# A fused attention and two-product MLP in fp32 pairs: the image's low half taken from PSUM, the weights' conversion moved into a PSUM bank, four units between products

## The chip, the cores and the metric

One core of a Trainium2 chip runs the whole program. The metric is the device time of one execution in microseconds; times below are from the hardware profiler or are medians of several executions.

## The reference

Attention with queries averaged in pairs, its output laid out as 2304 tokens of 512, and then a two-product MLP without a gate. Weights and activations are fp32 values (the weights come as float64).

```python
q_pool = q.reshape(B, H, S // 2, 2, D).mean(axis=3)          # B, H, S, D = 4, 8, 1152, 64
attn = softmax(q_pool @ k.T / sqrt(D))
x = (attn @ v).transpose(0, 2, 1, 3).reshape(B * S // 2, H * D)   # 2304 x 512
h = x @ w_in                                                  # 512 x 2048
g = s * maximum(h, 0) ** 2 + b                                # s, b: one number each
out = g @ w_out                                               # 2048 x 512
```

## The kernel before

**Pairs.** To keep fp32 accuracy every matrix operand is a pair: a high part rounded to the engine's fp32r format, and a low part, what rounding took away. A product is three multiplications: high by high, high by low, low by high.

**Attention** runs first, for 32 heads, and ends near 572 us. The change leaves it as it is. Its output `x` goes to DRAM (`xd`), block by block.

**The MLP** works on 9 blocks of 256 tokens and 16 slices of 128 hidden columns. A *unit* is one block by one slice, 144 in all, in three passes over the blocks: slices 0 to 2, 3 to 8, 9 to 15 (`SW`). One block in one pass is a *sweep*: 3, 6 or 7 units. For each unit, on the engine in brackets:

- `mm1`, the **first product** (TensorE): 12 multiplications of 256 columns into the left half of a PSUM bank `h`;
- **relu** L277 (ScalarE): `r`;
- **square** L267 (VectorE): `t` = max(h, 0) times `r`, into SBUF;
- the **image**, twice (ScalarE): L270 makes `gh`, s t + b rounded to fp32r; L271 makes the same in full, `g`, in the right half of the bank `h`;
- **rest** L274 (VectorE): `gl` = `g` - `gh`; it is the last reader of the bank `h`, of which there are four;
- `mm2`, the **second product** (TensorE, L287): 6 multiplications of 512 columns into two banks `y`, `DEPTH` = 3 units after the first product.

After the last unit of a sweep `store` takes `y` out: L294 (ScalarE) in the first pass, L296 (VectorE, with the sum of the pass before, `yq`) in the others.

**The order** is written out by hand. After each first product and after each half of a second product the loop calls `pace`, one *tick*, so a unit has three. `later(k, fn)` puts a step k ticks later; steps that are due are issued in the order in which they were put down. The engines run what they were given in that order. `MO` = (2, 3, 6) places square, image and rest.

**The split of x.** At a sweep's start the next block's `x`, already fetched (`xr`, one buffer, on SP's queue), is copied to its high part (L198, ScalarE, one tick later) and the low part is taken (L239, GpSimd, two ticks later). After that the block after the next is fetched.

**The conversion of weights.** Slices 3 to 15 of both matrices are converted from float64 while the first units run, 26 *chunks* of 128 by 512, one every `WB` = 6 ticks; slices 9 to 15 are wanted first at unit 81. A chunk's steps, at the ticks in `STB`, are: L144 and L145 (ScalarE) from the two words of a double; L149, L151, L152 (VectorE), clamp, shift and merge, each needing the one before; L155 (VectorE) and L156 (ScalarE, the high part); L160, L163, L166 (GpSimd): the scaled low word, the difference from the high part, their sum. All tiles are in SBUF, and each exists twice.

Of the kernel before, what the change touches and what calls it, by code (L numbers as in the profile page):

```python
# [38 lines left out]
XT = (1, 2, 3, 5, 8)  # L39
SW = (3, 9)  # L40
CB, CP = 274, 18
WB = 6
# [12 lines left out]
def attention_moe_kernel(ctx: ExitStack, tc: tile.TileContext, q, k, v, w_in, w_out, s_in, b_in, out):  # L55
# [46 lines left out]
            wo_hi[f] = oh[:, i, :]  # L102
            wo_lo[f] = ol[:, i, :]

    def conversions(pool, stage, f0, f1, bufs, stages):

# [29 lines left out]
        def narrow(i):  # L136
            _, hi, lo, name = chunks[i]
            words = raw.pop(i).rearrange("p c (n w) -> p c n w", w=2)
            high, low = words[:, :, :, 1].bitcast(F32), words[:, :, :, 0].bitcast(U32)
            hm, ab, A, R = (tmp(t, name) for t in ("whm", "wab", "wA", "wR"))  # L140
            hmi, abi, Ai, top = (t.bitcast(I32) for t in (hm, ab, A, high))

            def s0():
                nc.scalar.activation(hm, high, AF.Abs)  # L144
                nc.scalar.activation(R, low, AF.Copy, scale=2.0 ** -52)  # L145

            def s1():

                nc.vector.tensor_scalar(out=hm, in0=hm, scalar1=W_MIN, scalar2=W_MAX, op0=ALU.max, op1=ALU.min)  # L149

                nc.vector.tensor_scalar(out=abi, in0=hmi, scalar1=0x07FFFFFF, scalar2=3, op0=ALU.bitwise_and, op1=ALU.logical_shift_left)  # L151
                nc.vector.scalar_tensor_tensor(out=Ai, in0=top, scalar=-0x40000000, in1=abi, op0=ALU.bitwise_and, op1=ALU.bitwise_or)  # L152

            def s2():
                nc.vector.tensor_scalar(out=abi, in0=Ai, scalar1=-0x800000, scalar2=None, op0=ALU.bitwise_and)  # L155
                nc.scalar.activation(hi, A, AF.Copy)  # L156
# [61 lines left out]
    class Moe:  # L218
# [33 lines left out]
        def mm1(self, blk, f):  # L252
            xh, xl = self.x[blk]
            h = self.hp.tile([P, 512], F32, tag="h", name=f"h{blk}_{f}")
            n = 0
# [468 lines left out]
```

## Time and profile before

| what | value |
| --- | --- |
| median of 3 runs | 1018.68 us (1016.87 to 1018.93) |
| the profiled execution's own time | 1018.46 us |
| its span, first to last instruction | 1016.6 us |
| TensorE busy | 927.6 us, 91% |
| VectorE busy | 651.7 us, 64% |
| ScalarE busy | 686.6 us, 68% |
| GpSimd busy | 379.6 us, 37% |

PE is TensorE's multiplications, PEld its weight loads, DVE VectorE, ACT ScalarE, POOL GpSimd, SP the queue that issues the transfers. A row `out<-in` names the tiles without their numbers; `x4` counts instructions; what stands in brackets behind a row is the idle time before it and what ended it. In the list of waits the columns are total us, times, longest us. Busy shares average over stages; here the attention (up to 572 us) and the three passes of the MLP have different limits.

### The profile page before, as it was taken

How to read it: one execution, taken by the hardware profiler on the slowest of the kernel's cores; microseconds unless marked ns; L12 is line 12 of the kernel's file. 1: busy time of each engine (PE TensorE's matmuls, PEld its weight loads, DVE VectorE, ACT ScalarE, POOL GpSimd, SP SyncE). 2: the span in 40 equal slices, each digit the busy share in tenths (PEclk: the TensorE clock that was granted, in tenths of full speed). 3: DMA queues.
4: the chain of work that ended last, by engine and by line, in shares of the span. 5: the costliest groups of instructions: out<-in, count | busy, mean ns of one | idle time of the engine just before them, and what ended most of it. 6: DMA issues, size and time to landing. Idle time of an engine off the chain costs nothing.

```text
span 1016.6 us, 16051 instructions
## 1 busy us (share of the span) xinstructions
PE 927.6 (91%) x5680; PEld 818.0 (80%) x5680; DVE 651.7 (64%) x1191; ACT 686.6 (68%) x1278; POOL 379.6 (37%) x270
## 2 busy tenths in 40 slices
PE   4899999999999999989989987888889999999998
PEld 2778888888788878878878876767779999999997
DVE  5677777777778777877876378777783333333333
ACT  2577677767776787778777777876666555555553
POOL 5323223423342335235523288786772010011000
PEclk9999999999999999999999999999999999999999
DMA  8769765876587669766762245554442313213211
GB/s 166 137 117 190 152 124 108 179 158 126 114 165 161 122 136 184 167 125 136 175 154 55 74 148 186 185 187 145 141 149 84 125 63 114 73 63 92 96 43 42
DMA packets 255311, 131.15 MB, mean 129 GB/s; under 512 B 203776, under 2 KB 227328, under 8 KB 255232
## 3 DMA queue, kind: packets, MB, share of 16 engines
q1 hardware_dynamic: 248064, 130.06, 53.5%
q10 hardware_dynamic: 7168, 0.08, 0.4%
q8 instruction: 45, 0.74, 0.3%
q14 instruction: 34, 0.28, 0.1%
HBM read 68.68 MB, written 18.87 MB: 86 GB/s over the span
## 4 chain that ended last, share of the span: by engine, by line
PE 56%; DVE 20%; ACT 12%; issue 5%; DMA 2%; POOL 2%; ACTq 1%; SPq 0%; DVEq 0%; POOLq 0%
PE y L287 13%; PE h L258 12%; PE s L472 10%; PE o L501 7%; PE m L442 6%; DVE pl L484 4%; DVE pm L443 3%; PE o L511 3%; PE o L509 3%; ACT s L482 3%; ACT ph L480 3%; PE o L507 2%; DVE wAo L152 2%; DVE wAi L152 2%; DVE wabo L151 1%
## 5 line engine op out<-in xcount | busy, mean ns | idle before, releaser
L443 DVE TENSOR_REDUCE pm<-m 128x1 f32<-128x384 f32 x432 | 230.1, 548 | 51.1 <-PE m L442 44.0
L472 PE MATMUL s<-qq,kk 128*128 128x288 f32 x1152 | 208.0, 307 | 18.1 <-DVE pl L484 16.0
L258 PE MATMUL h<-x,wih 128*128 128x256 f32 x1152 | 213.3, 282 | 3.7 <-POOL x L239 3.7
L472 PEld LDWEIGHTS s<-qq,kk 128*128 128x128 f32 x1152 | 170.8, 190 | 40.9 <-DVE pl L484 16.6
L258 PEld LDWEIGHTS h<-x,wih 128*128 128x128 f32 x1152 | 186.9, 189 | 16.6 <-POOL x L239 5.5
L484 DVE TENSOR_TENSOR pl<-s,ph 128x576 fp32r<-128x576 f32 x176 | 132.5, 753 | 85.9 <-ACT s L482 85.8
L442 PE MATMUL m<-kh,qz 128*128 128x384 f32 x384 | 167.5, 446 | 21.5 <-DVE pm L443 21.0
L267 DVE SCALAR_TENSOR_TENSOR t<-h,r 128x256 f32<-128x256 f32 x144 | 60.7, 421 | 168.3 <-ACT r L277 168.3
L480 ACT ACTIVATE ph<-s 128x576 fp32r<-128x576 f32 x176 | 113.9, 647 | 79.6 <-PE s L472 78.6
L258 PE MATMUL h<-x,wil 128*128 128x256 f32 x576 | 162.2, 282 | 0.0
L239 POOL TENSOR_TENSOR x<-xr,x 128x1024 fp32r<-128x1024 f32 x27 | 66.0, 2444 | 229.6 <-ACT x L198 229.6
L501 PE MATMUL o<-pe,vf 128*128 128x288 f32 x448 | 144.7, 407 | 0.0
L287 PE MATMUL y<-woh,gl 128*128 128x512 f32 x288 | 115.7, 402 | 24.9 <-DVE gl L274 24.9
L270 ACT ACTIVATE gh<-t,sb 128x256 fp32r<-128x256 f32 x144 | 86.2, 598 | 65.9 <-DVE t L267 65.8
L482 ACT ACTIVATE s<-s 128x576 f32<-128x576 f32 x176 | 114.2, 649 | 0.0
L287 PE MATMUL y<-wol,gh 128*128 128x512 f32 x288 | 113.2, 393 | 0.0
L287 PE MATMUL y<-woh,gh 128*128 128x512 f32 x288 | 112.8, 392 | 0.0
L258 PEld LDWEIGHTS h<-x,wil 128*128 128x128 f32 x576 | 109.5, 190 | 0.0
L442 PEld LDWEIGHTS m<-kh,qz 128*128 128x128 f32 x384 | 74.7, 195 | 43.1 <-DVE pm L443 33.9
L507 PE MATMUL o<-ph,vv 128*128 128x288 f32 x352 | 107.4, 305 | 0.2 <-POOL vv L200 0.2
L509 PE MATMUL o<-ph,vl 128*64 128x288 f32 x352 | 104.5, 297 | 0.9 <-POOL vl L417 0.9
L511 PE MATMUL o<-pl,vv 128*128 128x288 f32 x352 | 103.6, 294 | 0.0
(73 smaller groups left out, 1481.9 us busy)
## 6 DMA issues: line engine op xcount, KB each, us to landing
kk<-kh SPq DMA_DIRECT2D x32, 576.0 KB, 5.7
kraw<-in_k_dram SPq DMA_DIRECT2D x64, 144.0 KB, 3.1
qraw<-in_q_dram SPq DMA_DIRECT2D x128, 72.0 KB, 2.5
vf<-in_v_dram SPq DMA_DIRECT2D x32, 288.0 KB, 4.4
kk<-kT SPq DMA_DIRECT2D x32, 288.0 KB, 3.3
qq<-qh SPq DMA_DIRECT2D x64, 144.0 KB, 5.6
xr<-xd SPq DMA_DIRECT2D x18, 512.0 KB, 4.0
wsti<-in_moe_w_in_dram SPq DMA_DIRECT2D x16, 512.0 KB, 4.8
```

Of the source, the lines that this page charges most:

```text
L258: nc.tensor.matmul(h[:, :TB], st[:, c, :], mv[:, c, :], start=(n == 0), stop=(n == 3 * NC - 1))
L287: nc.tensor.matmul(y[:, :DM], st[:, ts_], mv, start=(first and n == 0), stop=(last and n == 2))
L442: nc.tensor.matmul(ps[:, :KB], st, khs[p][:, e * KB:(e + 1) * KB], start=True, stop=True)
L443: nc.vector.tensor_reduce(out=pms[p][:, col, e:e + 1], in_=ps[:, :KB], axis=AX.X, op=ALU.max)
L472: nc.tensor.matmul(ps[:, a, :HALF], kk[:, i, j * P:(j + 1) * P], qq[:, i, a], start=(i == 0), stop=(i == 1))
L480: nc.scalar.activation(ph, ps[:, :, :HALF], AF.Exp, scale=SCALE)
L482: nc.scalar.activation(ps[:, :, :HALF], ps[:, :, :HALF], AF.Exp, scale=SCALE)
L484: fresh.append(lambda: eng.tensor_tensor(out=pl, in0=ps[:, :, :HALF], in1=f32(ph), op=ALU.subtract))
L501: nc.tensor.matmul(o[:, :HALF], vfs[hd % 2][:, j], ph[:, a], start=first, stop=last)
L507: nc.tensor.matmul(o[:, :HALF], vv[:, j], ph[:, a], start=first, stop=False)
L509: nc.tensor.matmul(o[0:D, :HALF], vl[:, j], ph[:, a], start=False, stop=False)
L511: nc.tensor.matmul(o[:, :HALF], vv[:, j], pl[:, a], start=False, stop=last)
```

## The change

- **The image's difference.** The square now multiplies by s as well and is written into the right half of the bank `h` (L273). One image is left (L276, `gh` = square + b), reading PSUM; the rest (L279) adds b to the square in PSUM and subtracts `gh` in one operation. The second image and the SBUF tile `t` are gone.
- **The conversion on one PSUM bank.** ScalarE writes |high word| into a bank of its own (L148); clamp, shift and merge (L156, L158, L159) work in place there; the exponent mask (L162) and the high part (L163) are read from it; the difference from the high part (L170) moves from GpSimd to VectorE. The scaling of the low word (L152) moves from ScalarE to GpSimd. There is one such bank, for 26 chunks.
- **Wider steps.** The first 12 chunks come every 7 ticks and the others every 11 (`WB`), and a chunk's steps are closer together (`STB`).
- **Banks and distance.** Three `h` banks for four, and four units between a unit's products (`DEPTH`), with five buffers of `gh` and `gl`.

```diff
-WB = 6
+WB = (7, 11)
-STB = (0, 2, 4, 6, 8, 10)
+STB = (0, 2, 3, 5, 5, 8)
-DEPTH = 3
+DEPTH = 4
...
+            bank = None if psum is None else psum.tile([P, 512], F32, tag="w", bufs=1, name=f"w{name}").rearrange("p (c f) -> p c f", c=NC)
+            hm, bits, full = (hm, ab, A) if psum is None else (bank, bank, bank)
+            eng = nc.gpsimd if psum is None else nc.vector
...
-                nc.scalar.activation(R, low, AF.Copy, scale=2.0 ** -52)
+                if psum is None:
+                    nc.scalar.activation(R, low, AF.Copy, scale=2.0 ** -52)
+                else:
+                    nc.gpsimd.tensor_scalar(out=R, in0=low, scalar1=2.0 ** -52, scalar2=0.0, op0=ALU.mult, op1=ALU.add)
...
-                nc.gpsimd.tensor_tensor(out=A, in0=A, in1=f32(hi), op=ALU.subtract)
+                eng.tensor_tensor(out=A, in0=full, in1=f32(hi), op=ALU.subtract)
...
-            t = self.p.tile([P, TB], F32, tag="t", bufs=2, name=f"t{blk}_{f}")
-            g = h[:, TB:]
+            t = h[:, TB:]
...
-                nc.vector.scalar_tensor_tensor(out=t, in0=h[:, :TB], scalar=0.0, in1=r, op0=ALU.max, op1=ALU.mult)
-                nc.scalar.activation(gh, t, AF.Identity, bias=sb[:, 1:2], scale=sb[:, 0:1])
-                nc.scalar.activation(g, t, AF.Identity, bias=sb[:, 1:2], scale=sb[:, 0:1])
+                nc.vector.scalar_tensor_tensor(out=t, in0=h[:, :TB], scalar=sb[:, 0:1], in1=r, op0=ALU.mult, op1=ALU.mult)
+                nc.scalar.activation(gh, t, AF.Identity, bias=sb[:, 1:2])
...
-                nc.vector.tensor_tensor(out=gl, in0=g, in1=f32(gh), op=ALU.subtract)
+                nc.vector.scalar_tensor_tensor(out=gl, in0=t, scalar=sb[:, 1:2], in1=f32(gh), op0=ALU.add, op1=ALU.subtract)
...
-    ps_h = ctx.enter_context(tc.tile_pool(name="ps_h2", reuse_waits="tile", bufs=4, space=PSUM))
+    ps_h = ctx.enter_context(tc.tile_pool(name="ps_h2", reuse_waits="tile", bufs=3, space=PSUM))
+    ps_w = ctx.enter_context(tc.tile_pool(name="ps_w2", reuse_waits="tile", bufs=1, space=PSUM))
...
-        if count % WB == 0:
+        if wait == 0:
             weights_b()
-        count += 1
+            begun += 1
+            wait = WB[0 if begun <= 2 * (SW[1] - SW[0]) else 1]
+        wait -= 1
```

How the instructions move, at three places. The first is VectorE in the first pass, one chunk between units: before (`whm`, `wab`, `wA` are the chunk's tiles in SBUF),

```order
L267 SCALAR_TENSOR_TENSOR t_1_7049<-h_1_7035,r_1_7048 128x256
L149 TENSOR_SCALAR whmi_7055<-whmi_7055 128x512
L151 TENSOR_SCALAR wabi_7056<-whmi_7055 128x512
L152 SCALAR_TENSOR_TENSOR wAi_7057<-wsti_6965,wabi_7056 128x512
L274 TENSOR_TENSOR gl_0_7013<-h_0_6997,gh_0_7012 128x256
L155 TENSOR_SCALAR wabi_7056<-wAi_7057 128x512
L267 SCALAR_TENSOR_TENSOR t_2_7089<-h_2_7075,r_2_7088 128x256
L274 TENSOR_TENSOR gl_1_7051<-h_1_7035,gh_1_7050 128x256
```

and now, where `wo` is the bank and `h_0_6957`, `h_1_7007` are units 9 and 10:

```order
L273 SCALAR_TENSOR_TENSOR h_0_6957<-h_0_6957,sb,r_0_6970 128x256
L279 SCALAR_TENSOR_TENSOR gl_2_6942<-h_2_6927,sb,gh_2_6941 128x256
L156 TENSOR_SCALAR wo_6987<-wo_6987 128x512
L158 TENSOR_SCALAR wo_6987<-wo_6987 128x512
L159 SCALAR_TENSOR_TENSOR wo_6987<-wsto_6902,wo_6987 128x512
L162 TENSOR_SCALAR wabo_6984<-wo_6987 128x512
L273 SCALAR_TENSOR_TENSOR h_1_7007<-h_1_7007,sb,r_1_7020 128x256
L279 SCALAR_TENSOR_TENSOR gl_0_6972<-h_0_6957,sb,gh_0_6971 128x256
L170 TENSOR_TENSOR wAo_6985<-wo_6987,woh_6656 128x512
```

The mask L162 now stands directly behind the three steps, ahead of the next square and of the rest of unit 9, and a fifth operation, L170, follows that rest.

The second is ScalarE at a sweep's first unit in the first pass. Before,

```order
L277 ACTIVATE r_0_7259<-h_0_7246 128x256
L156 ACTIVATE wih_6651<-wAi_7218 128x4x128
L198 ACTIVATE x_6_6_7244<-xr_6_7151 128x1024
L270 ACTIVATE gh_0_7261<-t_0_7260,sb 128x256
L271 ACTIVATE h_0_7246<-t_0_7260,sb 128x256
L277 ACTIVATE r_1_7297<-h_1_7284 128x256
```

and now:

```order
L282 ACTIVATE r_0_7317<-h_0_7304 128x256
L205 ACTIVATE x_7_7_7302<-xr_7_7220 128x1024
L299 ACTIVATE yo_True_False<-y_0_7249 128x512
L299 ACTIVATE yo_True_False<-y_1_7250 128x512
L148 ACTIVATE wo_7345<-wsto_7254 128x512
L276 ACTIVATE gh_0_7318<-h_0_7304,sb 128x256
L282 ACTIVATE r_1_7364<-h_1_7351 128x256
```

With one unit more between the products, the two copies of `y` (L294, now L299) fall between the split of `x` and the image of the sweep's first unit; before they stood two units later.

The third is GpSimd, between two splits of `x`. Before,

```order
L239 TENSOR_TENSOR x_4_4_6996<-xr_4_6902,x_4_4_6995 128x1024
L160 TENSOR_TENSOR wRo_6970<-wRo_6970,wabo_6968 128x512
L163 TENSOR_TENSOR wAo_6969<-wAo_6969,woh_6653 128x512
L166 TENSOR_TENSOR wol_6654<-wAo_6969,wRo_6970 128x512
L160 TENSOR_TENSOR wRi_7058<-wRi_7058,wabi_7056 128x512
L163 TENSOR_TENSOR wAi_7057<-wAi_7057,wih_6651 128x512
L239 TENSOR_TENSOR x_5_5_7116<-xr_5_7025,x_5_5_7115 128x1024
```

and now:

```order
L246 TENSOR_TENSOR x_4_4_6956<-xr_4_6872,x_4_4_6955 128x1024
L167 TENSOR_TENSOR wRo_6986<-wRo_6986,wabo_6984 128x512
L152 TENSOR_SCALAR wRi_7067<-wsti_6982 128x512
L173 TENSOR_TENSOR wol_6657<-wAo_6985,wRo_6986 128x512
L246 TENSOR_TENSOR x_5_5_7075<-xr_5_6992,x_5_5_7074 128x1024
```

The subtraction is gone from this queue, a scaling stands in it, and fewer of them lie between two splits.

Lines move by the added text: L258 to L265 (first product), L277 to L282 (relu), L287 to L292 (second product), L294 and L296 to L299 and L301, L198 to L205, L239 to L246, L160 and L166 to L167 and L173. The prediction uses the old numbers for rows of the kernel before and the new ones for what is new.

## Rows read from the trace of the kernel before

**Rows 1.** The page's strip of 40 slices of 25.4 us: busy tenths of TensorE.

```profile
PE   4899999999999999989989987888889999999998
```

**Rows 2.** Busy time of each engine in two stretches (columns: stretch, its length, PE, PEld, DVE, ACT and POOL busy us with instruction counts, granted clock, DMA share, GB/s).

```profile
572.00:760.00 188.00, 159.40 (x980) 135.65 (x979) 144.25 (x220) 137.36 (x274) 140.17 (x91) 1.00 0.49 159
765.00:1005.00 240.00, 240.00 (x1546) 218.87 (x1545) 80.51 (x198) 134.55 (x272) 28.85 (x12) 1.00 0.25 80
```

**Rows 3.** The chain of waits in order of time (start, us, what): the first product with which the chain stays on TensorE, and the last two pieces.

```profile
759.55 1.41 PE h L258 x12
...
1006.10 1.43 PE h L258 x12
1007.53 5.47 PE y L287 x24
```

**Rows 4.** The timeline of TensorE (start, us): the first product of the MLP, and a wait in unit 6.

```profile
572.05 0.40 PE L258 MATMUL h<-x,wih 128*128 128x256 f32 x2
...
586.68 0.39 PE L258 MATMUL h<-x,wih 128*128 128x256 f32 x1 [0.41 <-POOL x L239]
```

**Rows 5.** What TensorE waited for from 572 to 760 us (total us, times, longest us).

```profile
PE y L287 <- DVE gl L274: 24.9, 17, 1.7
PE h L258 <- POOL x L239: 3.7, 6, 0.9
```

**Rows 6.** The timeline of VectorE (start, us): one chunk of the conversion.

```profile
643.88 0.43 DVE L149 TENSOR_SCALAR whmo<-whmo 128x512 f32<-128x512 f32 x1
644.41 1.33 DVE L151 TENSOR_SCALAR wabo<-whmo 128x512 int32<-128x512 int32 x1
645.83 1.60 DVE L152 SCALAR_TENSOR_TENSOR wAo<-wsto,wabo 128x512 int32<-128x512 int32 x1
647.35 0.41 DVE L274 TENSOR_TENSOR gl<-h,gh 128x256 fp32r<-128x256 f32 x1
647.69 0.41 DVE L155 TENSOR_SCALAR wabo<-wAo 128x512 int32<-128x512 int32 x1
```

**Rows 7.** Shortest, median and longest time in ns of VectorE's operations, by line, and the first and last start. In L484, L267, L274 and L296 one operand (`s`, `h`, `h`, `y`) lies in PSUM; in the others all lie in SBUF.

```profile
L151 DVE TENSOR_SCALAR wabo<-whmo x16: 426/1330/1405, 419.6 to 755.0; 128x512 int32<-128x512 int32 x16
...
L152 DVE SCALAR_TENSOR_TENSOR wAo<-wsto,wabo x16: 691/693/1643, 420.1 to 756.4; 128x512 int32<-128x512 int32 x16
...
L155 DVE TENSOR_SCALAR wabo<-wAo x16: 409/792/2283, 422.8 to 758.2; 128x512 int32<-128x512 int32 x16
...
L484 DVE TENSOR_TENSOR pl<-s,ph x175: 739/757/759, 27.5 to 567.2; 128x576 fp32r<-128x576 f32 x175
...
L267 DVE SCALAR_TENSOR_TENSOR t<-h,r x144: 386/424/426, 575.4 to 1008.0; 128x256 f32<-128x256 f32 x144
...
L274 DVE TENSOR_TENSOR gl<-h,gh x144: 407/414/425, 577.6 to 1009.6; 128x256 fp32r<-128x256 f32 x144
...
L296 DVE TENSOR_TENSOR yo_False_True<-y,yq x18: 681/691/692, 859.9 to 1013.0; 128x512 f32<-128x512 f32 x18
```

**Rows 8.** Groups of VectorE's instructions from 572 to 760 us (busy us, mean ns of one; idle before): a chunk's four operations, for `w_out`.

```profile
L152 DVE SCALAR_TENSOR_TENSOR wAo<-wsto,wabo 128x512 int32<-128x512 int32 x13 | 15.3, 1179 | 1.1
...
L151 DVE TENSOR_SCALAR wabo<-whmo 128x512 int32<-128x512 int32 x13 | 13.8, 1058 | 1.3
...
L155 DVE TENSOR_SCALAR wabo<-wAo 128x512 int32<-128x512 int32 x13 | 12.9, 992 | 0.0
...
L149 DVE TENSOR_SCALAR whmo<-whmo 128x512 f32<-128x512 f32 x13 | 11.0, 846 | 1.8
```

**Rows 9.** Groups of ScalarE's instructions over the whole run (busy us, mean ns of one; idle before).

```profile
L270 ACT ACTIVATE gh<-t,sb 128x256 fp32r<-128x256 f32 x144 | 86.2, 598 | 65.9 <-DVE t L267 65.8
...
L277 ACT ACTIVATE r<-h 128x256 f32<-128x256 f32 x144 | 54.4, 378 | 59.5 <-PE h L258 58.9
...
L156 ACT ACTIVATE woh<-wAo 128x512 fp32r<-128x512 f32 x16 | 10.1, 630 | 17.6 <-DVE wAo L152 15.3 <-POOL wAi L163 2.4
...
L294 ACT ACTIVATE yo_True_False<-y 128x512 f32<-128x512 f32 x18 | 9.6, 583 | 0.0
```

**Rows 10.** Groups of GpSimd's instructions over the whole run (the same columns).

```profile
L166 POOL TENSOR_TENSOR wol<-wAo,wRo 128x512 fp32r<-128x512 f32 x16 | 22.6, 1414 | 0.9
...
L163 POOL TENSOR_TENSOR wAo<-wAo,woh 128x512 f32<-128x512 f32 x16 | 21.8, 1362 | 0.0
...
L200 POOL TENSOR_SCALAR vv<-vf 128x576 fp32r<-128x576 f32 x32 | 21.5, 673 | 96.7 <-DMA vf<-in_v_dram 51.0 <-PE m L442 16.7 <-PE o L511 14.8
L160 POOL TENSOR_TENSOR wRo<-wRo,wabo 128x512 f32<-128x512 f32 x16 | 21.4, 1338 | 10.3 <-DVE wabo L155 9.8 <-DMA wsti<-in_moe_w_in_dram 0.4
```

**Rows 11.** The split of `x`: from the timelines of SP, ScalarE and GpSimd (start, us), and the fetches of 512 KB from 570 to 760 us (count, size, median us from issue to landing).

```profile
577.49 0.91 SPq L230 DMA_DIRECT2D xr<-xd  x2
...
583.09 1.06 ACT L198 ACTIVATE x<-xr 128x1024 fp32r<-128x1024 f32 x1 [1.13 <-DMA xr<-xd]
...
584.23 2.40 POOL L239 TENSOR_TENSOR x<-xr,x 128x1024 fp32r<-128x1024 f32 x1 [5.37 <-ACT x L198]
...
616.95 2.67 POOL L239 TENSOR_TENSOR x<-xr,x 128x1024 fp32r<-128x1024 f32 x1 [1.18 <-ACT x L198]
...
627.47 2.41 POOL L239 TENSOR_TENSOR x<-xr,x 128x1024 fp32r<-128x1024 f32 x1 [2.24 <-ACT x L198]
...
xr<-xd SPq DMA_DIRECT2D x8, 512.0 KB, 4.1
```

More of the change, by code (lines that the diff above doesn't have):

```diff
@@ L103, in weight_tiles, with conversions @@
             wo_lo[f] = ol[:, i, :]
-    def conversions(pool, stage, f0, f1, bufs, stages):
+    def conversions(pool, stage, f0, f1, bufs, stages, psum=None):
         weight_tiles(pool, f0, f1)
@@ L139, in narrow @@
             high, low = words[:, :, :, 1].bitcast(F32), words[:, :, :, 0].bitcast(U32)
[L140 to L141 removed]
+            hm, ab, A, R = (tmp(t, name) for t in ("whm", "wab", "wA", "wR")) if psum is None else (None, *(tmp(t, name) for t in ("wab", "wA", "wR")))
+            bank = None if psum is None else psum.tile([P, 512], F32, tag="w", bufs=1, name=f"w{name}").rearrange("p (c f) -> p c f", c=NC)
+            hm, bits, full = (hm, ab, A) if psum is None else (bank, bank, bank)
+            hmi, biti, abi, fulli, top = (t.bitcast(I32) for t in (hm, bits, ab, full, high))
+            eng = nc.gpsimd if psum is None else nc.vector
             def s0():
                 nc.scalar.activation(hm, high, AF.Abs)
[L145 removed]
+                if psum is None:
+                    nc.scalar.activation(R, low, AF.Copy, scale=2.0 ** -52)
+                else:
+                    nc.gpsimd.tensor_scalar(out=R, in0=low, scalar1=2.0 ** -52, scalar2=0.0, op0=ALU.mult, op1=ALU.add)
             def s1():
                 nc.vector.tensor_scalar(out=hm, in0=hm, scalar1=W_MIN, scalar2=W_MAX, op0=ALU.max, op1=ALU.min)
[L151 to L152 removed]
+                nc.vector.tensor_scalar(out=biti, in0=hmi, scalar1=0x07FFFFFF, scalar2=3, op0=ALU.bitwise_and, op1=ALU.logical_shift_left)
+                nc.vector.scalar_tensor_tensor(out=fulli, in0=top, scalar=-0x40000000, in1=biti, op0=ALU.bitwise_and, op1=ALU.bitwise_or)
             def s2():
[L155 to L156 removed]
+                nc.vector.tensor_scalar(out=abi, in0=fulli, scalar1=-0x800000, scalar2=None, op0=ALU.bitwise_and)
+                nc.scalar.activation(hi, full, AF.Copy)
             def s3():
@@ L260, in mm1, with image @@
             r = self.p.tile([P, TB], F32, tag="r", bufs=2, name=f"r{blk}_{f}")
-            t = self.p.tile([P, TB], F32, tag="t", bufs=2, name=f"t{blk}_{f}")
-            g = h[:, TB:]
-            gh = self.p.tile([P, TB], F32R, tag="gh", bufs=4, name=f"gh{blk}_{f}")
-            gl = self.p.tile([P, TB], F32R, tag="gl", bufs=4, name=f"gl{blk}_{f}")
+            t = h[:, TB:]
+            gh = self.p.tile([P, TB], F32R, tag="gh", bufs=DEPTH + 1, name=f"gh{blk}_{f}")
+            gl = self.p.tile([P, TB], F32R, tag="gl", bufs=DEPTH + 1, name=f"gl{blk}_{f}")
             def square():
-                nc.vector.scalar_tensor_tensor(out=t, in0=h[:, :TB], scalar=0.0, in1=r, op0=ALU.max, op1=ALU.mult)
-            def affine():
-                nc.scalar.activation(gh, t, AF.Identity, bias=sb[:, 1:2], scale=sb[:, 0:1])
-                nc.scalar.activation(g, t, AF.Identity, bias=sb[:, 1:2], scale=sb[:, 0:1])
+                nc.vector.scalar_tensor_tensor(out=t, in0=h[:, :TB], scalar=sb[:, 0:1], in1=r, op0=ALU.mult, op1=ALU.mult)
+            def image():
+                nc.scalar.activation(gh, t, AF.Identity, bias=sb[:, 1:2])
             def rest():
-                nc.vector.tensor_tensor(out=gl, in0=g, in1=f32(gh), op=ALU.subtract)
+                nc.vector.scalar_tensor_tensor(out=gl, in0=t, scalar=sb[:, 1:2], in1=f32(gh), op0=ALU.add, op1=ALU.subtract)
                 self.g[blk, f] = gh, gl
             nc.scalar.activation(r, h[:, :TB], AF.Relu)
-            for at, fn in zip(MO, (square, affine, rest)):
+            for at, fn in zip(MO, (square, image, rest)):
                 later(at, fn)
@@ L664, in attention_moe_kernel @@
     work = [(i, blk, f, fs) for i, (blk, fs) in enumerate(sweeps) for f in fs]
-    count = 0
+    wait = 0
+    begun = 0
     def pace():
-        nonlocal count
-        if count % WB == 0:
+        nonlocal wait, begun
+        if wait == 0:
             weights_b()
-        count += 1
+            begun += 1
+            wait = WB[0 if begun <= 2 * (SW[1] - SW[0]) else 1]
+        wait -= 1
         tick()
```

2 lines of the change are left out of this document (1 added, 1 removed).

## The prediction

> **What bounds the kernel now.** First the 40 slices: TensorE is nearly full, but stands at 7 or 8 tenths in all of slices 24 to 30 (585 to 762 us), and at 9 or more from there to the last but one [rows 1]. The two stretches beside each other say the same: from 572 to 760 us PE is busy for 159.4 of 188 us, from 765 to 1005 for all 240, at full granted clock in both [rows 2]. Then the chain of waits in order of time: its late part is PE alone, a first product (1.43 us) and a second one (5.47 / 4 = 1.37 us) in turn, so 2.80 us for a unit [rows 3]. Unit 55 begins at 759.55 and the last one, 143, at 1006.10, which is 88 x 2.80 us: there no engine but PE matters. The first unit begins at 572.05 [rows 4]; 144 units at 2.80 us are 403.2 us and would end at 975.25, but the last product ends at 1013.00 [rows 3]. So **37.75 us are lost, and all before unit 55**, while the weights are converted. The list of PE's waits there names the owner: 24.9 us for `gl`, which VectorE writes, and 3.7 us for `x`, which GpSimd writes [rows 5]; the remaining 9 us I put down to the refill of PE around these waits.
>
> Why `gl` is late stands in VectorE's timeline of one conversion [rows 6]: between the clamp L149 and `gl` the two steps L151 and L152 take 1.33 and 1.60 us. Over the whole run the same lines have a shortest time of 0.43 and 0.69 us; L155 goes from 0.41 to 2.28 [rows 7]. The operations with one operand in PSUM keep their time in every instance (L484 739 to 759 ns, L267 386 to 426, L274 407 to 425, L296 681 to 692) though GpSimd is busy for 140 of the 188 us [rows 2, 7]. So what stretches is what works on SBUF alone, beside GpSimd. A chunk costs VectorE 0.85 + 1.06 + 1.18 + 0.99 = 4.1 us in the mean [rows 8], against 0.43 + 0.43 + 0.69 + 0.41 = 1.96 undisturbed [rows 6, 7].
>
> **The change, part by part.** The attention's instructions are as before, so everything up to 572.05 stays, and so do the 3.6 us from the last product to the end of the span (1016.6 - 1013.0) and the 1.86 us between the span and that execution's own time, 1018.46. (The median shown is 0.22 us above it.) PE's own work stays too: `DEPTH` moves one second product from the front to the end.
>
> *The conversion on a PSUM bank.* VectorE gets five operations for four, all with a PSUM operand. The nearest row is L296, 512 elements with one PSUM operand: 0.69 us, never stretched [rows 7]. Bounds: 0.43 us, a step undisturbed on SBUF, and 1.38, twice L296, if reading and writing the same bank took turns (no row writes PSUM from VectorE). I take 0.69. A step that needs the one before it starts about 0.09 us after its end (L149 ends at 644.31, L151 starts at 644.41 [rows 6]); one that needs nothing starts 0.08 before the end (L274 ends at 647.76, L155 starts at 647.69). So a chunk is 3 x 0.78 + 2 x 0.61 = 3.56 us, less than the 4.1 it costs now. The Trainium skill ("VectorE: DVE Perf Modes", section "Why PSUM operands drop a tier") speaks against the move: an fp32 operation with a PSUM operand loses the double rate that SBUF gives it. By that rule alone, set against undisturbed times, the 26 chunks would add 26 x 1.6 = 42 us to VectorE; by the rows the double rate is not had beside GpSimd, and the load falls.
>
> *VectorE's load.* A unit adds square and rest, 0.42 us each and 0.08 less from start to start where nothing waits [rows 6, 7]: 0.7. Twelve chunks come every 7 ticks, 7/3 units or 6.53 us: 3.56 + 2.33 x 0.7 = 5.2 us, 80%. Fourteen come every 11 ticks, 10.27 us: 3.56 + 3.67 x 0.7 + 0.84 for the second pass's L296 = 7.0 us, 68%. VectorE no longer sets the rate.
>
> *ScalarE* loses the second image of each unit and a conversion of each chunk; the image left has one pointer operand and a PSUM source, between L277 and L270, 0.38 to 0.60 us [rows 9]. Off the path, hence no term. *GpSimd* gives away a subtraction of 1.36 us (L163) for an operation with one input, between 0.67 us (L200) and that same 1.36; I take L200, the only one-input row of its size [rows 10]; per 6.53 us it does that, L160 and L166 (0.67 + 1.34 + 1.41) and, per 8.4 us sweep of three units, 2.4 for `x` [rows 11]: about 81%. Each also queues behind a wait: `x` stands behind L167, which waits for VectorE's `wab`.
>
> *What is late next.* (a) **The start.** `x` of block 2 is fetched at 577.49, lands for ScalarE at 583.09, and is split by 586.63 [rows 11]; unit 6's second multiplication starts at 586.68 for that [rows 4], so unit 6 at 586.44. Nothing here is changed. Until then PE can do 6 first products and, with four units between products, 2 second ones: 11.3 of 14.4 us. **Loss 3.1.** (b) **Three `h` banks.** The first product of unit m+3 needs the rest of unit m, 8.4 us after unit m began. Without disturbance: product 1.43, relu at 2.0, square 2.4, image 3; rest stands behind the next unit's square and is done near 5.8, so 2.6 us of slack. At a sweep's first unit ScalarE puts the split of `x` and two L294 (1.05 + 2 x 0.58, [rows 9]) ahead of the image, and a chunk's four VectorE steps (3 us) may stand ahead of the rest too. For unit 9 both meet. It begins at 586.44 + 8.4 = 594.8. The `x` fetched at 586.7 lands 4.1 later and is split by 594.4 (1.05 + 2.4 + 0.2 between); the next is fetched then, in two pieces, some 4.9 us by the 4.1 of one piece and the 5.6 of two above, and ScalarE copies it from 599.3 to 600.4, then L294, the chunk's L148 and L294 again to 602, whence L156 to L162 on VectorE to 604.6, square and rest to 605.4, against 594.8 + 8.4 = 603.2. **Loss 2.1**, after which `x` is no longer late: its own loop is 4.1 landing, 1.05, 2.4 and 0.2 between, 7.8 of 8.4 us. (c) The same meeting with `x` in time, about 3 of the other sweeps at 0.4 us (the chain above with `x` in time puts the rest near 8.8 after the unit's start instead of 8.4); and in the second pass, where L296 stands between a chunk's three steps and the rest at a block's end, rest 6.6 us after that unit's start for 5.6 wanted, nine block ends with 2 ticks of 11 each, 1.6 times 1 us: **2.8**. Each is an estimate from these rows.
>
> Sum: 572.05 + 403.2 + 3.1 + 2.1 + 2.8 + 3.6 + 1.86 = **988.7 us**, 30 us or 2.9% less.
>
> **The rivals.** A. *Only the start is lost*: 980.7 (the sum without losses) + 3.1 = 983.8. For it: every mean load is under 82%. Against: in-order queues with 2.6 us of slack and bursts of 3 us. 12% (982 to 985). B. *The `x` loop keeps bounding the first sweep*: its splits come 10.5 us apart in mid-sweep (616.95 to 627.47), and 9.2 at the start (from the fetch at 577.49 to the end of the next split, 586.63, [rows 11]), and 0.6 us of slack goes with any queueing on GpSimd. At 9.8 us for seven sweeps it is 7 x 1.4 = 9.8 more: 998. 11%. C. *The stretch stays*, because it comes from something else than SBUF operands: the chunk is 3.56 + 2.1 (4.1 - 1.96) = 5.7, a period 7.3 against 6.53, twelve times 0.8: 998. Speaking against it: 480 unstretched instances [rows 7]. [...] 4%. D. *Turns in the bank*: at 1.38 us for the three steps that read and write it, and 0.84 for a square, a period is 3 x 1.38 + 2 x 0.69 + 2.33 x 1.26 = 8.5, later 3.67 x 1.26 + 5.5 + 0.84 = 11: 12 x 2 + 14 x 0.7 = 34 more than A, 1018: no change. 3%. E. **Slower**: the single conversion bank. The next chunk's L148, ahead of relus on ScalarE, waits for the last chunk's L170 on VectorE, which stands behind squares that wait for relus. The bank is held for L148 0.63 (by L156, [rows 9]), three steps 2.34, ScalarE's copy the same 0.63 and 0.1, square and rest twice 1.4 at most, L170 0.69: 5.8 of 6.53 us. If each hand-over instead takes a turn of the unit and the holding grows to 10.8 us, the twelve lose 4.27 each and the fourteen 0.53: 983.8 + 58.7 = 1042. It decides against the change from 9.6 us on. 4%.
>
> **How the numbers follow.** The forecast, losses of 4 to 14 us, 985 to 995, has 66%. With A and most of B and C the range is **983 to 1000**; left out are D, E and the ends of A and B, some 14%. About 0.2%, 2 us, is what a measurement can tell from no change: faster 0.93 (66 + 12 + 11 + 4), same 0.03 (D), slower 0.04 (E).
>
> **What would show it.** Right: PE at 9 or more from slice 24 on; VectorE's L156 to L170 near 0.69 us with shortest and longest within a few per cent; PE's wait for `gl` gone, small waits for `h` banks (L279) and `x` (L246), some 5 us together; the last stage at 2.80 us a unit; unit 6 at 586.4. Wrong: L156 to L159 near 1.4 us (D), or stretched (C); ScalarE's L148 waiting long for L170 (E); PE waiting for L246 in most of the nine first sweeps (B). A span of the attention other than 572 us would break the sum's first term.

## The result, and the profile after

The changed kernel takes **995.2 us** (median of four runs, 991.9 to 996.4) against 1018.5 for the kernel before (median of four, 1016.9 to 1018.9): ratio **0.977**, 95% interval 0.974 to 0.980. The profiled execution is the fastest of its four, 991.93 us, with a span of 990.1 at a mean granted clock of 0.996. The prediction was 988.7, in 983 to 1000.

The page's strip for TensorE, against [rows 1]: the tenths of 7 and 8 in slices 24 to 30 have all become 9.

```profile
PE   4799999999999998989899999999999999999998
```

The same two kinds of stretch as in [rows 2] (length, then PE, PEld, DVE, ACT, POOL busy us, granted clock, DMA share, GB/s). The first pass is not yet full, but everything behind it is.

```profile
572.00:665.00 93.00, 86.23 (x548) 75.44 (x547) 67.40 (x124) 55.62 (x118) 64.05 (x48) 1.00 0.57 179
665.00:980.00 315.00, 314.25 (x2019) 286.03 (x2018) 163.60 (x328) 123.39 (x270) 83.35 (x58) 1.00 0.32 106
```

The chain of waits in order of time, against [rows 3]: it is PE alone from 660.58 (unit 30) on but for one piece at unit 74. Before, that was so from 759.55 on, unit 55.

```profile
660.58 1.68 PE h L265 x12
...
784.83 1.69 PE h L265 x12
...
979.73 6.83 PE y L292 x30
```

What TensorE waited for, against [rows 5]. The waits of the second product for `gl` are gone; what is left is the first product waiting for one of the three `h` banks, by this list for the rest L279 or the image L276.

```profile
PE h L265 <- DVE gl L279: 6.2, 8, 1.4
PE h L265 <- ACT gh L276: 1.2, 1, 1.2
```

VectorE's operations of the conversion in ns, shortest, median and longest, against [rows 7] (first two: clamp and shift, then the merge, the top bits, and the subtraction taken from GpSimd; last the square). Nothing is stretched any more.

```profile
L156 DVE TENSOR_SCALAR wo<-wo x13: 690/691/700, 584.6 to 801.8; 128x512 f32<-128x512 f32 x13
L158 DVE TENSOR_SCALAR wo<-wo x13: 699/699/700, 585.3 to 802.6; 128x512 int32<-128x512 int32 x13
L159 DVE SCALAR_TENSOR_TENSOR wo<-wsto,wo x13: 695/695/696, 586.0 to 803.3; 128x512 int32<-128x512 int32 x13
L162 DVE TENSOR_SCALAR wabo<-wo x13: 680/691/692, 586.8 to 804.1; 128x512 int32<-128x512 int32 x13
L170 DVE TENSOR_TENSOR wAo<-wo,woh x13: 681/692/694, 588.2 to 805.5; 128x512 f32<-128x512 f32 x13
L273 DVE SCALAR_TENSOR_TENSOR h<-h,sb,r x144: 454/493/494, 575.3 to 980.2; 128x256 f32<-128x256 f32 x144
```

The sum closes: first product at 571.92, 403.2 for 144 units, 3.6 from the last product (986.56) to the end of the span, 1.8 around it; so **11.4 us are lost** where before lost 37.75. *Lost by a unit*, below, is that unit's start in PE's timeline less the start of unit 0 and 2.80 us for each unit between (1.43 for the three or four at the front that have no second product); counted in this way the change loses 11.3 and before 37.6.

### The profile page after: what moved, and what is told of

Same layout as the page of the kernel before. It is cut to its first block, busy times and chain, and to the rows that moved or that the text cites. A ratio compares the mean times of both kernels' runs of the same rounds, so it can differ in the third digit from the quotient of the medians.

```text
span 990.1 us, 16006 instructions
## 1 busy us (share of the span) xinstructions
PE 921.4 (93%) x5680; PEld 818.6 (83%) x5680; DVE 654.0 (66%) x1217; ACT 588.2 (59%) x1108; POOL 354.6 (36%) x270
## 4 chain that ended last, share of the span: by engine, by line
PE 65%; DVE 12%; ACT 8%; issue 4%; DMA 4%; POOL 3%; ACTq 1%; SPq 0%; DVEq 0%; POOLq 0%
PE h L265 17%; PE y L292 16%; PE s L477 11%; PE o L506 8%; PE m L447 6%; DVE pl L489 4%; DVE pm L448 4%; PE o L514 3%; PE o L516 3%; PE o L512 2%; ACT s L487 2%; ACT ph L485 2%; POOL x L246 1%; DMA xr<-xd 1%; DVE qT L406 1%
## 5 line engine op out<-in xcount | busy, mean ns | idle before, releaser
L265 PE MATMUL h<-x,wih 128*128 128x256 f32 x1152 | 213.1, 283 | 7.5 <-DVE gl L279 6.2
L265 PEld LDWEIGHTS h<-x,wih 128*128 128x128 f32 x1152 | 185.7, 189 | 22.7 <-DVE gl L279 6.9
L265 PE MATMUL h<-x,wil 128*128 128x256 f32 x576 | 162.2, 282 | 0.0
L273 DVE SCALAR_TENSOR_TENSOR h<-h,sb,r 128x256 f32<-128x256 f32 x144 | 70.5, 489 | 131.2 <-ACT r L282 131.2
L246 POOL TENSOR_TENSOR x<-xr,x 128x1024 fp32r<-128x1024 f32 x27 | 64.9, 2405 | 174.3 <-ACT x L205 174.3
L282 ACT ACTIVATE r<-h 128x256 f32<-128x256 f32 x144 | 55.5, 385 | 110.6 <-PE h L265 110.6
L292 PE MATMUL y<-wol,gh 128*128 128x512 f32 x288 | 113.1, 393 | 0.0
L292 PE MATMUL y<-woh,gl 128*128 128x512 f32 x288 | 112.9, 392 | 0.0
L292 PE MATMUL y<-woh,gh 128*128 128x512 f32 x288 | 112.7, 391 | 0.0
L265 PEld LDWEIGHTS h<-x,wil 128*128 128x128 f32 x576 | 109.6, 190 | 0.0
L276 ACT ACTIVATE gh<-h,sb 128x256 fp32r<-128x256 f32 x144 | 68.2, 473 | 64.5 <-DVE h L273 63.9
```

Source lines behind the costliest of these rows:

```text
L246: nc.gpsimd.tensor_tensor(out=xl, in0=xr, in1=f32(xh), op=ALU.subtract)
L292: nc.tensor.matmul(y[:, :DM], st[:, ts_], mv, start=(first and n == 0), stop=(last and n == 2))
```

## The experiments

Two theories stood at the start. **Bank** (the prediction's): VectorE's stretched steps make `gl` late, and the PSUM operands end that. **Queue**: a chunk is one lump of 3 to 4 us in VectorE's queue, with a unit's square and rest behind it; it costs whenever too few units follow before the next lump, and the pace of the chunks is what the gain comes from. What each run lost by unit 27 (the first pass, 12 chunks) and from there to unit 81 (the second pass, 14 chunks), in its profiled execution:

| run | ticks to a chunk | first pass | second pass | ratio to before, 95% |
|---|---|---|---|---|
| before | 6, 6 | 18.6 | 19.0 | 1 |
| the change | 7, 11 | 8.0 | 3.3 | 0.977 (0.974 to 0.980) |
| e1, the change again | 7, 11 | 10.0 | 3.4 | 0.976 (0.975 to 0.978) |
| e2, image alone | 6, 6 | 20.4 | 16.0 | 0.999 (0.998 to 1.000) |
| e3, bank alone | 6, 6 | 16.3 | 18.8 | 0.998 (0.997 to 0.999) |
| e4, all but the bank | 7, 11 | 11.5 | 2.8 | 0.978 (0.977 to 0.980) |
| e5, pace alone | 7, 11 | 15.9 | 2.3 | 0.982 (0.980 to 0.984) |
| e6, all but the pace | 6, 6 | 17.4 | 18.4 | 1.000 (0.999 to 1.001) |
| e7, GpSimd emptied | 6, 6 | 12.2 | 4.0 | 0.981 (0.979 to 0.983) |
| e8, four `h` banks | 7, 11 | 9.8 | 0.4 | 0.975 (0.973 to 0.976) |
| e9, bank alone, four `h` banks | 6, 6 | 16.0 | 18.0 | 0.997 (0.996 to 0.999) |
| e10, second pass at 7 | 7, 7 | 10.2 | 9.2 | 0.979 (0.977 to 0.982) |
| e11, second pass at 9 | 7, 9 | 10.3 | 2.6 | 0.975 (0.973 to 0.977) |
| e12, three units between products | 7, 11 | 6.0 | 1.5 | 0.970 (0.968 to 0.972) |

Some of this is TensorE's clock. In six of these executions the granted clock falls to 0.5 (1.2 GHz, the lower of its two levels) for 3.41 us at a time, each time within 1.6 us of the end of a wait of TensorE of 0.7 to 3.8 us: in the first pass twice in e2 and once in e5 and e11, in the second pass once in e6 and e9 and twice in e10. Each fall costs some 1.7 us (in e10 1.65 at unit 31, and 1.67 at units 45 and 46). Before, the change, e1, e3, e4, e7, e8 and e12 have none in these passes.

**e1: the change once more**, unaltered, to see how far two measurements of it differ.

> The changed kernel once more, unaltered. Its four executions so far lie 4.4 us apart (991.9 to 996.4), and the only profile is of the fastest. If the spread is of the executions, not of the build, this gives 992 to 997 again and a second profile, whose lost time from the first to the last product should be 11 to 16 us against 11.3 in the first; if the slower executions lose in the attention, the first product of the MLP will begin later than 571.9.

993.4 us (992.5 to 994.5). Its profiled execution lost 13.4 us by unit 81 for 11.3: executions of this kernel differ by about 0.4%, and the first pass is where these two differ.

**e2: the image alone**, in the kernel before.

```diff
-            t = self.p.tile([P, TB], F32, tag="t", ...)
-            g = h[:, TB:]
+            t = h[:, TB:]
-                nc.scalar.activation(gh, t, AF.Identity, bias=sb[:, 1:2], scale=sb[:, 0:1])
-                nc.scalar.activation(g, t, AF.Identity, bias=sb[:, 1:2], scale=sb[:, 0:1])
+                nc.scalar.activation(gh, t, AF.Identity, bias=sb[:, 1:2])
```

> The kernel before with the image's part alone: the square into the h bank, one image, the rest from PSUM. Four h banks, three units between products, conversion in SBUF every 6 ticks, all as before. Contention (VectorE's conversion steps are stretched beside GpSimd, and PSUM operands end that): the stretched steps stay, ScalarE is off the path, so 1008 to 1017. Image (ScalarE's second image is what delays gl): 995 to 1004.

1017.2 us, no change, though ScalarE is freed of 144 operations of some 0.55 us. At six ticks ScalarE was off the path, as predicted; beside the wide pace the image was not tried alone.

**e3: the conversion's bank alone** (three `h` banks and the new steps `STB` with it), six ticks to a chunk.

```diff
-STB = (0, 2, 4, 6, 8, 10)
+STB = (0, 2, 3, 5, 5, 8)
+            bank = None if psum is None else psum.tile([P, 512], F32, tag="w", bufs=1, ...)
+            hm, bits, full = (hm, ab, A) if psum is None else (bank, bank, bank)
-    ps_h = ... bufs=4 ...
+    ps_h = ... bufs=3 ...
+    ps_w = ... bufs=1 ...
```

> The conversion on the PSUM bank (one bank, three h banks, the steps' new places) but still every 6 ticks, with both images and three units between products as before. Contention: VectorE's chunk falls from 4.1 to 3.6 us unstretched, at 5.6 us a chunk it is 91% loaded, so part of the 37 us stays: 996 to 1006. Pace (the gain is that of the wider steps, the bank is incidental): no gain, 1013 to 1020.

1016.0 us: 0.2% gained, where the Bank theory wants nearly all. Its steps are unstretched (the merge, shortest, median and longest in ns):

```profile
L159 DVE SCALAR_TENSOR_TENSOR wo<-wsto,wo x13: 695/695/696, 588.6 to 753.3; 128x512 int32<-128x512 int32 x13
```

And yet TensorE waits as long as before, now for the `h` bank (total us, times, longest us):

```profile
PE h L265 <- DVE gl L281: 26.2, 31, 1.6
```

Why shows in VectorE's timeline of e3, from one square to the next but one (start, us; in brackets the idle time ahead and what ended it):

```profile
641.01 0.42 DVE L274 SCALAR_TENSOR_TENSOR t<-h,r 128x256 f32<-128x256 f32 x1 [1.10 <-ACT r L284]
641.54 0.70 DVE L156 TENSOR_SCALAR wo<-wo 128x512 f32<-128x512 f32 x1
642.27 0.70 DVE L158 TENSOR_SCALAR wo<-wo 128x512 int32<-128x512 int32 x1
643.00 0.69 DVE L159 SCALAR_TENSOR_TENSOR wo<-wsto,wo 128x512 int32<-128x512 int32 x1
643.61 0.42 DVE L281 TENSOR_TENSOR gl<-h,gh 128x256 fp32r<-128x256 f32 x1
643.94 0.68 DVE L162 TENSOR_SCALAR wabo<-wo 128x512 int32<-128x512 int32 x1
645.36 0.69 DVE L170 TENSOR_TENSOR wAo<-wo,woh 128x512 f32<-128x512 f32 x1 [0.73 <-ACT woh L163]
645.97 0.42 DVE L274 SCALAR_TENSOR_TENSOR t<-h,r 128x256 f32<-128x256 f32 x1
646.30 0.41 DVE L281 TENSOR_TENSOR gl<-h,gh 128x256 fp32r<-128x256 f32 x1
647.81 0.42 DVE L274 SCALAR_TENSOR_TENSOR t<-h,r 128x256 f32<-128x256 f32 x1 [1.10 <-ACT r L284]
```

The chunk holds VectorE from 641.54 to 645.97, less 0.33 for the rest in its midst: **4.10 us**, what it cost before [rows 8]; counted alike over all 26 chunks, waits included, the mean is 4.0 us in both. The prediction's 3.56 left out the 0.73 in which VectorE stands still for ScalarE's copy L163, with a square behind; 22 of the 26 chunks have that wait here. And the lump is part of a loop: the rest behind three steps (643.61) frees the `h` bank, the first product starts at once (644.08 in PE's timeline, after 0.88 of waiting), the relu follows, VectorE waits 1.10 for it. Square to square takes 6.80 us for two units that TensorE needs 5.60 for: 1.2 us lost for this chunk, as for most others, though VectorE is busy for only 28.46 of 40 us:

```profile
620.00:660.00 40.00, 34.68 (x214) 29.59 (x214) 28.46 (x54) 29.11 (x59) 28.18 (x22) 1.00 0.56 180
```

**e4: the change without the bank**; the conversion is in SBUF with GpSimd's subtraction, with four `h` banks.

```diff
-    weights_b = conversions(wb, wstage, SW[0], NF, 2, STB, ps_w)
+    weights_b = conversions(wb, wstage, SW[0], NF, 2, STB)
```

> The changed kernel with the conversion back in SBUF and on GpSimd as before (four h banks), but with the 7 and 11 ticks, the steps' new places, the new image and four units between products. Contention: the steps stretch again to about 4.1 us a chunk; VectorE and GpSimd are each at 92% in the first 28 units, so 1000 to 1010. Pace: as good as the changed kernel, 992 to 997.

995.7 us, beside the repeat's 993.4; the intervals overlap. The four steps of a `w_out` chunk are stretched here, but to 956 + 641 + 767 + 499 ns in the mean, 2.9 us together (from 572 to 830 us), and those of a `w_in` chunk to 3.2: less than the 3.5 of the bank's five. At the wide pace the bank is worth between nothing and 0.4%: the upper end is e8 below, which has the bank and four `h` banks like this run, and one `y` bank less.

**e5: the pace alone**, in the kernel before.

```diff
-WB = 6
+WB = (7, 11)
+            wait = WB[0 if begun <= 2 * (SW[1] - SW[0]) else 1]
```

> The kernel before with nothing changed but the ticks between chunks: 7 for the first twelve, then 11. Queue (a chunk is one lump of VectorE work ahead of a unit's rest; what it costs PE is won back only if enough ticks follow): the 14 later chunks cost nothing, as in the changed kernel's units 31 to 73, the first 12 cost up to 1.4 us each as now, and the start 3: 995 to 1003. Contention or bank: the stretched steps are all still there, 1008 to 1017.

999.5 us: **1.8% of the 2.3% that the change gains** come from two numbers. By the table most of it is the second pass (19.0 lost, then 2.3); the first pass, at seven ticks for six, gives 2.7. On SBUF the pace does two things at once: the lumps come further apart, and in the second pass they are shorter too (the four steps take 2.5 us in the mean for 3.8 before; in the first pass 4.2 for 4.1). This run does not tell the two apart. The change and the next run do.

**e6: everything but the pace.**

```diff
-WB = (7, 11)
+WB = (6, 6)
```

> The changed kernel with 6 ticks between all chunks again; bank, image, four units and three h banks as changed. Queue: 26 chunks lose about 1 to 1.3 us each, 1006 to 1016. Distance and image (four units between products and the shorter image chain give the gain): 992 to 999.

1018.2 us, no change at all. The five steps of a chunk on the bank take 3.47 us in the mean here and in the change alike, yet at six ticks the second pass loses 18.4 us and at eleven 3.3. So the distance between the chunks is enough by itself, and without it the bank, the image, the depth and the new steps together gain nothing. Late loads of the weights are no rival to the lump: ScalarE waits for them at six ticks here (7.8 us in all, and unit 44 with the fall of the clock behind it loses 5.6), but in e3 only 0.8 us in all, and before not at all, for the same loss. Beside the pace they do gain: e5's 0.982 becomes 0.977 in the change, and 0.970 in e12 below.

**e7: GpSimd emptied** in the kernel before, six ticks: the three operations of a chunk of slices 3 to 15 are left out, and one that fills the low half with zeros stands for them.

```diff
-                nc.gpsimd.tensor_tensor(out=R, in0=R, in1=ab, op=ALU.mult)
-                nc.gpsimd.tensor_tensor(out=A, in0=A, in1=f32(hi), op=ALU.subtract)
-                nc.gpsimd.tensor_tensor(out=lo, in0=A, in1=R, op=ALU.add)
+                nc.gpsimd.memset(f32(lo), 0.0)
```

> The kernel before, every 6 ticks, with GpSimd's three operations of a chunk in slices 3 to 15 left out and one memset of the low part in their place (the weights' low parts are zero, which is left out of the result). If the stretching beside GpSimd is what makes the lump too long, VectorE's chunk falls to 2.0 us, under the slack of 2.6, and most of the 37 us go: 982 to 992. If only the ticks between chunks count: 1010 to 1018.

998.4 us, between the two ranges expected. So the contention that the prediction saw is real and long enough to matter at six ticks: where GpSimd leaves it alone, a chunk is 1.96 us, its first three steps hold the rest up by 1.54 (694.63 to 696.17 in VectorE's timeline; 2.07 in e3), and the second pass loses 4.0. The first pass still loses 12.2: GpSimd still splits `x` there, the steps take 3.2 us in the mean (before, 4.1), and TensorE waits for `x` (5.0 us in all) more than for `gl` (3.0). At six ticks the bank is no cure: it removes the stretch and puts back a fifth operation, a slower rate and a wait for ScalarE, and a chunk is 4.10 us again (e3).

**e8: four `h` banks** and three for `y` in the change.

```diff
-    ps_h = ... bufs=3 ...      ps_y = ... bufs=4 ...
+    ps_h = ... bufs=4 ...      ps_y = ... bufs=3 ...
```

> The changed kernel with four h banks and three y banks instead of three and four. PE's waits for the rest (L279, 6 to 7 us, and the refill behind them) are waits for an h bank; with a fourth the rest may come 2.8 us later. If the banks bind: 985 to 989, the lost time in units 9 to 30 gone but for the split of x. If something behind the bank binds (x, or gl itself): 991 to 995.

991.9 us (991.4 to 992.6); beside the change and its repeat the intervals overlap, so the missing fourth `h` bank costs some 0.2%. By the table it is the second pass that gains (0.4 us lost for 3.3).

**e9: the bank alone with four `h` banks**, six ticks: e3 with the banks of e8.

> The conversion on the PSUM bank with its new steps, six ticks to a chunk as before, both images of the square as before, three units between products, but with four h banks and three y banks (the other bank experiment at six ticks had three and four). Question: did the missing h bank eat what the bank of the conversion gains? Bank theory: yes; the steps keep 0.69 us, PE's 26 us of waiting for an h bank go, and the time falls to 1003 or below. Queue theory (a chunk is 3.5 us of VectorE work in one lump ahead of a unit's square and rest, and six ticks are two units, too short to win it back): the wait only changes its name, from the h bank (L265) to gl at the second product (L292), some 1 us for every chunk; 1008 to 1017.

1014.6 us: the missing bank hid 0.1%, no more than the intervals of the two runs. The wait changed its name, though not only as expected: 6.4 us for `gl`, and 14.0 for the two lines that empty a `y` bank, of which there are now three.

**e10 and e11: other paces in the second pass.**

```diff
-WB = (7, 11)
+WB = (7, 7)          # e10;   (7, 9) in e11
```

> The changed kernel with seven ticks to a chunk in the second pass too, instead of eleven. Seven ticks are 2.33 units, so a chunk meets another phase of the unit each time; the conversion then ends near unit 61. Queue theory: what counts is the time between lumps; 6.53 us for 3.5 + 2.33 x 0.8 + 0.8 of VectorE work leaves little, some 0.3 to 0.5 us a chunk are lost in units 31 to 61, the time is 996 to 1001. Phase theory (six ticks lose because they are exactly two units, so that every chunk falls on the same spot before the rest): seven are as good as eleven, nothing lost after unit 31, 992 to 995.

> The changed kernel with nine ticks to a chunk in the second pass instead of eleven: exactly three units, so again every chunk meets the same phase, but with 8.4 us between them. Queue theory: 3.5 + 3 x 0.8 + 0.8 us of VectorE work in 8.4 leaves 1.7 us, a lump is won back before the next; nothing lost after unit 31, 992 to 995. Phase theory: the fixed phase costs each of the 14 chunks again, some 0.5 to 1.2 us: 1000 to 1010.

997.6 and 992.4 us; TensorE from 665 to 745 us, first e10, then e11:

```profile
665.00:745.00 80.00, 77.74 (x478) 69.59 (x477) 64.72 (x119) 38.47 (x84) 47.74 (x40) 0.96 0.53 172
```

```profile
665.00:745.00 80.00, 80.00 (x515) 72.47 (x515) 60.47 (x113) 38.70 (x86) 42.27 (x34) 1.00 0.50 164
```

Nine ticks lose as little as eleven, though they are again a whole number of units, as six are. So it is the time between lumps and not the phase: 5.60 us fail and 8.40 are enough. What 6.53 us cost is not shown. The profiled execution of e10 is the slowest of its four (1000.6 us; the others 994.8 to 998.6), and its 9.2 us do not come chunk by chunk: 2.0 go at unit 30, which costs the change 1.6 as well, 2.3 at unit 44, before which ScalarE waited 2.00 us for the chunk's own load, and 3.3 at the lower clock right behind these two waits; all else is 1.5. The second fall (stretch, length, busy us as above, granted clock, DMA share, GB/s):

```profile
708.90:712.30 3.40, 3.40 (x12) 2.82 (x11) 2.94 (x7) 1.76 (x4) 2.30 (x3) 0.51 0.80 282
```

**e12: three units between the products** in the change.

```diff
-DEPTH = 4
+DEPTH = 3
```

> The changed kernel with three units between a unit's two products instead of four. The prediction gave the fourth unit no gain of its own. Queue theory: the fourth unit is 2.8 us more for the rest behind a lump; without it PE waits for gl at the second product (L292) in the first pass where it now waits for an h bank, some 2 to 6 us more: 995 to 999. Bank theory: with three h banks the h bank is asked for earlier than gl in either case, so three units lose nothing: 992 to 995.

**987.4 us** (985.1 to 989.1), ratio 0.970 (0.968 to 0.972): the best of all, and against both theories. The fourth unit costs 0.6 to 0.7%. PE's timeline shows one place. With three banks the fourth first product waits 1.20 us in either kernel; in the change, where five first products follow each other, the sixth waits too. First the change, then e12:

```profile
577.58 0.47 PE L265 MATMUL h<-x,wih 128*128 128x256 f32 x2 [1.20 <-ACT gh L276]
...
580.52 0.39 PE L292 MATMUL y<-woh,gh 128*128 128x512 f32 x1
...
582.38 0.50 PE L265 MATMUL h<-x,wih 128*128 128x256 f32 x2 [0.30 <-DVE gl L279]
```

```profile
577.54 0.47 PE L265 MATMUL h<-x,wih 128*128 128x256 f32 x2 [1.20 <-ACT gh L276]
...
579.04 0.39 PE L292 MATMUL y<-woh,gh 128*128 128x512 f32 x1
...
580.44 0.40 PE L265 MATMUL h<-x,wih 128*128 128x256 f32 x2
```

With the late `x` at unit 7 that is 1.1 us from unit 3 to 7, in each of the four runs of the table with four units, three `h` banks and seven ticks (the change, e1, e10, e11), and 0.2 in e12. The change and e1 also lose 0.45 at unit 28 and 1.0 at unit 74, and e12 does not. The rest of what they lose more than e12 (3.8 us in the change, 5.9 in e1) lies in units 9 to 30. A candidate there is the end of a block, which a fourth unit puts into the first unit of the next sweep, where ScalarE splits `x`. ScalarE's timeline in e1 has the two copies L299 and the chunk's L163 between the split (after 3.57 us of waiting for its load) and the image; below it stands TensorE's first product of unit 15, right behind:

```profile
610.37 1.06 ACT L205 ACTIVATE x<-xr 128x1024 fp32r<-128x1024 f32 x1 [3.57 <-DMA xr<-xd]
611.34 0.58 ACT L299 ACTIVATE yo_True_False<-y 128x512 f32<-128x512 f32 x1
611.81 0.59 ACT L163 ACTIVATE wih<-wi 128x512 fp32r<-128x512 f32 x1
612.29 0.60 ACT L299 ACTIVATE yo_True_False<-y 128x512 f32<-128x512 f32 x1
612.76 0.49 ACT L276 ACTIVATE gh<-h,sb 128x256 fp32r<-128x256 f32 x1
```

```profile
614.58 0.47 PE L265 MATMUL h<-x,wih 128*128 128x256 f32 x2 [1.19 <-ACT gh L276]
```

In e12 the copies stand ahead of that wait (605.17), and from the split to the image it is 1.45 us (609.64 to 611.09) for 2.39 here. Units 15 and 16 cost e1 2.0 us, the change 0.2 and e12 0.1, so this is one third of e1's 5.9, and not what the change's own profile loses. There the chain shows the same order on ScalarE once more, with the chunk's lump behind it, ahead of the wait at unit 30:

```profile
655.71 1.07 ACT yo_True_False L299 x2
656.77 0.36 ACT gh L276
657.13 0.27 ACT r L282
657.41 0.54 ACT wo L148
657.98 0.71 DVE wo L156
...
660.14 0.40 DVE gl L279
```

But unit 30 costs e12 1.4 us as well, for 1.6 in the change. The two copies were not moved alone, so the candidate is not shown.

## Why the prediction was right, and where it was wrong

The number fell in its range and the direction was right, but the reason given as the main one was not what makes most of the gain. That the range was met is in part luck.

- **572.05 + 403.2, 3.6 and 1.86.** Right to 0.15 us each, and the last stage runs at 2.80 us a unit.
- **The conversion on the bank.** The durations were right: 0.69 for each of the five, never stretched, and no turns in the bank (rival D). The rule of the Trainium skill that was weighed there ("VectorE: DVE Perf Modes", section "Why PSUM operands drop a tier") is borne out: 0.69 for clamp and shift where the undisturbed step on SBUF takes 0.43. In the change a chunk, its waits included, is 3.56 us in the median, as predicted, and 3.7 in the mean, since in 9 of the 26 the subtraction waits 0.7 us or more, nearly always for ScalarE's copy; the prediction had that copy in rival E's sum for the bank, and not in VectorE's. The failed step is "less than the 4.1 it costs now" as what makes the gain. At six ticks the bank costs 4.10 as well and gains 0.2% (e3). At the wide pace the steps on SBUF take 3.0 us (e4, mean of all chunks), less than on the bank: in the second pass the stretch that the prediction took as given goes for the most part with the pace (2.4 us for the 3.8 before).
- **VectorE's load** of 80% and 68% was the wrong measure. In e3 VectorE is busy 71% of the time and TensorE loses some 1.2 us for every chunk. An in-order queue that is part of a loop with TensorE and ScalarE is judged by the loop's length (6.80 for 5.60 us), not by its busy share. The wider pace was in the sum as the period of that load alone, not as the lever that e5 and e6 show it to be; no rival said so.
- **(a) The start, 3.1.** 2.4 by unit 7, but by other terms: 1.37 at unit 3 and 0.5 at unit 5, whose first products wait for one of the three `h` banks, and only 0.5 at unit 7, where the late `x` was to take it all. Unit 6 begins at 585.31 and not at 586.4; in the kernel before, too, its first multiplication starts at 585.99, and only the second waits for `x`.
- **(b) Unit 9 and `x`, 2.1.** 1.9, but for two meetings: the one forecast costs 0.5 at unit 12 (its rest ends at 604.24 for the forecast 605.4), and the same one a sweep earlier 1.4 at unit 9, whose first product waits 1.15 us for the rest L279. Right in kind; the sum is luck.
- **(c) Other meetings, 2.8.** The mis-sized term: 7.0 us are lost behind unit 12, in units 16 to 30 above all and 1.0 at unit 74. e12 shows what was left out: `DEPTH` stands in (a), where it leaves TensorE less to do before `x` comes, but has no term behind it ("moves one second product from the front to the end"). Without it 7.5 us are lost in all, about the 8.0 predicted with it, but that is chance: 1.6 by unit 8 for the 3.1 of (a), 2.0 for (b), and 3.9 for the 2.8 of (c).
- **The image.** Off the path at six ticks: e2.
- **Rivals.** A, nothing lost but the start: refuted, 11.4. B, the `x` loop: in the change TensorE's list has no `x` among its longer waits, but in e4, on SBUF, it waits 6.5 us for L246, so the rival describes that neighbour. C and D: refuted by the durations. E, the single bank as a brake: at six ticks, too, the time is not above before (e6).

**What stays open:** how the 4 to 6 us of the fourth unit split; and which of the bank (with three `h` banks for four), the image and the new steps makes the 1.2% by which e12 (0.970) is ahead of the pace alone (e5, 0.982). No run takes these apart at the wide pace with three units between products: e4 was run with four, and the steps' new places were never tried alone.

## What to carry to other kernels

When work is interleaved into an engine's in-order queue, sum the whole loop that the engine closes with its partners, its waits for them included, and compare that with the time between two pieces; busy shares of 70% can hide a loop that is too long. Try the pace first: it is two numbers, and here it gave 1.8 of 2.3%. A deeper pipeline that shares the same buffers is no free margin; take each part of a change out alone, since one part may cost what another gains (0.970 without the fourth unit, 0.977 with it).

## What the runs showed of the hardware

- A VectorE operation on SBUF alone can last through several GpSimd instructions, not just one. In e7 the top bits L155, elsewhere 0.42 us, last until 638.45, 0.3 us after the end of three GpSimd instructions in a row (first VectorE, then GpSimd); four chunks of e7 show the same 3.29 or 3.30 us:

```profile
635.16 3.29 DVE L155 TENSOR_SCALAR wabi<-wAi 128x512 int32<-128x512 int32 x1
```

```profile
634.86 2.39 POOL L244 TENSOR_TENSOR x<-xr,x 128x1024 fp32r<-128x1024 f32 x1 [7.01 <-ACT x L203]
637.19 0.52 POOL L171 MEMSET wol<- 128x512 f32 x1
637.65 0.52 POOL L171 MEMSET wil<- 128x512 f32 x1
```

The Trainium skill ("SBUF — State Buffer", section "Who interferes with whom") describes an exclusive lock of VectorE and GpSimd, held for a whole instruction. The rows fit it: the loser stands still. That it lost the lock again to the two fills behind is read from the times alone. It does not lose it every time: in the kernel before, L155 at 639.27 lasts 2.29 us and ends 0.29 us after the split L239, though GpSimd's sum L166 follows that split at once.
- TensorE's granted clock fell to 0.5 (1.2 GHz) for 3.41 us right behind some waits and not behind others of the same length: behind 1.87 and 2.17 us in e10, and not behind 2.03 us in e7 (670.7) or 1.98 in e5 (671.9).
- The square into PSUM, with a pointer as its scalar, takes 0.49 us (L273) where the one into SBUF with a constant takes 0.42 [rows 7]: 10 us of VectorE's time over 144 units, of which none shows in the total (e2). Which of the two, place or pointer, costs it was not tried.
